# Block-sparse attention and a feed-forward layer on one core: a new issue order from a planner, with four token groups turned through DRAM instead of five and the weights loaded earlier

## The chip, the cores and the metric

The kernel runs on one core of one Trainium2 chip. The metric is the device time of one execution in microseconds (us). Engines are named as in the profile: PE multiplies matrices (PEld loads its stationary operand), DVE and ACT work on vectors, POOL is GpSimd, SP issues most DMAs.

## The reference

Four batches, eight heads, 768 tokens, 64 values per head. Attention is restricted to chunks of 32 keys: for each query the six chunks with the largest upper bound on the score are kept, then causally masked. The attended tokens (3072 of 512 values) go through a feed-forward layer of width 2048.

```python
k_min, k_max = k_chunks.min(axis=3), k_chunks.max(axis=3)
ub = sum(maximum(q * k_min, q * k_max), axis=-1)      # one bound for each query and chunk
ub = where(causal, ub, -1e9)
top_chunks = argsort(ub)[..., -6:]
scores = where(sel & causal_by_token, scale * q @ k.T, -1e9)
x = softmax(scores) @ v                               # tokens x (heads * 64)
h = x @ w_in                                          # 512 -> 2048
out = (h * clip(h + 3, 0, 6) / 6) @ w_out             # 2048 -> 512
```

## The kernel before

**Tiling.** Attention is done in 16 units: unit n has four heads of batch n // 4 (two "pairs" of heads) and one half of its tokens, 384. Units n % 4 of 0 and 1 are the first half, 2 and 3 the second. Two units make one group (batch, half) of 384 tokens, and the dense layers run on the eight groups (0,0), (0,1), (1,0) ... (3,1).

**A unit, in the kernel's names.** K and Q come in as `KS` and `QS`. In batch 0 they are loaded by quads (L237, rows of 256 bytes and more) and turned by PE into `KT`, `QT` (L377), which ACT, DVE and POOL copy out (`KL`, `QF`, L262 to L266). In the other batches four loads each (`load`, L246, rows of 128 bytes) put 32 x 32 blocks where DVE can turn them: `KF`, `QF` (L389). DVE reduces keys to chunk limits `KMA` (L402, L403), PE multiplies them with the queries into bounds `UBT` (L442), DVE turns these (`UB`, L447), finds the six largest (L459), builds the selection `SELA` (L464) and turns it to `MT` (L472), which is put beside the queries in `QLA` by L262 or L264. PE makes the scores `SPS` (L495 in batch 0, L498 after it), ACT the exponentials `PT` (L508), POOL cuts the triangle (L513), PE multiplies with the values `VB` into `PVP` (L529), and DVE divides by the sum (`RINV` L535, `Xb` L541). Values are loaded as `VS` (L252, batch 0) or `VT` (L257) and cast to `VB`.

**Turning the tokens.** The dense layer wants `Xb` with the model dimension on the partitions, as `XT`. There are two ways. By PE: 12 transposes into `XTP` (L550) and two DVE copies (L554). Through DRAM, for the groups in the list `WORDS`: two DVE transposes of pairs of bf16 as fp32 words (`BT`, L560), a store to DRAM (`BD`, L565), four loads (`BF`, L571), all issued by SP, and four POOL copies (L579).

**The dense layers.** `hidden` (L586): 16 steps of 4 matmuls into a bank `HP`; ACT makes `U` (L591), DVE makes `GT` (L594). `result` (L601): for each of three token tiles 16 matmuls into `OP`, then ACT or DVE scale to `OT` (L627, L629) and SP stores (L633). The last tile is done in two halves of columns (L609, L616, L622). `WIN` and `WOUT` (2 MB each in bf16, kept in SBUF) come in two halves each, `WIN0`, `WIN1`, `WOUT0`, `WOUT1`, by DMAs that POOL issues (L325, L328); before each one POOL copies one element of another load's tile (`seen`, L322), so that the load goes out only after that one has landed. The table `GATE` says which.

**What sets the order.** Nothing above is issued where it is written. Each step is given to a planner (`class Plan`) with an engine or a choice of engines, a length, a rank, the steps that it needs and the buffers that it takes and gives. `Plan.order` plays the schedule through, event by event, and each free engine takes the ready step of the lowest rank for which a buffer is free. The instructions are then issued in that order, engine by engine, and no engine changes its order at run time. The rank of a step is a formula in its unit or group plus an entry for that step's number in `SHIFT`. `FETCH` is a time at which the planner adds a delay to a DMA under way. For PE steps before 45 us of the plan in front of which PE stands idle in the plan, a few matmuls on the identity are put in ("fillers", L214).

```python
step = dict(..., rank=(rank + SHIFT.get(len(self.steps), 0), len(self.steps)), ...)
...
for st in sorted(steps, key=lambda x: x["rank"][:1] if e == "DMA" else x["rank"]):
```

Inputs of batch 0 are issued in the order `SEQ` (K0 Q0 K1 Q1 Q3 Q2 K2 V1 V0 V2 K3 V3, by unit). Loads on SP and stores on SP share one queue, whose instructions go out in the planned order too: a store that waits for its result holds the loads behind it.

Of the kernel before, what the change touches and what calls it, by code (L numbers as in the profile page):

```python
# [46 lines left out]
class Plan:  # L47
# [8 lines left out]
    FETCH = 15.3, 1.35  # L56
# [36 lines left out]
    def order(self, **busy):  # L93
# [20 lines left out]
        while events:  # L114
            now, _, done, own = heapq.heappop(events)
            if done:
                behind(done, own)
                if not own:
                    for held in done["give"]:
                        held[1] -= 1  # L120
                        if not held[1]:
                            self.room[held[0]].append(held[2])
                            opened[held[0], held[2]] = now
            for e, steps in ready.items():
                if free[e] > now + 1e-9:
                    continue
                for st in sorted(steps, key=lambda x: x["rank"][:1] if e == "DMA" else x["rank"]):
                    if "engine" in st:
                        steps.remove(st)
                    elif self.sooner(st, e, free, now):  # L130
                        continue
                    elif self.room_for(st):
                        steps.remove(st)
                        for held in st["take"]:
                            held[2] = self.take(held[0])
                        st["idle"] = now - max([free[e], *(opened.get((held[0], held[2]), 0.0) for held in st["take"])])
                        out.append(st)
                        begin = now
                        if e == "POOL" or e == "DVE" and st["port"]:
                            begin = max(now, port["DVE" if e == "POOL" else "POOL"])  # L140
                            port[e] = begin + st["lengths"][e]
                        begin = max(begin, locks.get(st["lock"], 0.0))
                        if e == "PE":
                            begin += 0.1 * (st["tiles"] != tiles)
                            tiles = st["tiles"]
                        length = st["lengths"][e]
                        if e == "PE" and begin < self.COLD:
                            length *= 1.9
                        if e == "DMA":
                            weights = max(free["WT"] - now, 0.0) + sum(x["lengths"]["WT"] for x in ready["WT"])  # L150
                            length = min(length / st["share"], weights + max(length - st["share"] * weights, 0.0))
                            if now <= self.FETCH[0] < now + length:
                                length += self.FETCH[1]
                        st["at"], st["engine"], st["length"] = begin, e, length
                        free[e] = begin + st["length"]
                        if st["lock"]:
                            locks[st["lock"]] = free[e] + 0.12
                        n += 2
                        heapq.heappush(events, (free[e], n, st, True))
                        heapq.heappush(events, (free[e] + self.BEHIND[e], n + 1, st, False))  # L160
                        break
# [10 lines left out]
def kernel(  # L172
# [345 lines left out]
    WORDS = [(1, 1), (2, 0), (2, 1), (3, 0), (3, 1)]  # L518
# [119 lines left out]
    GATE = dict(I0="V3", I1="I0", O0="K4", O1="I1")  # L638
# [15 lines left out]
    def arrive(engine, issue, length, run, after=(), take=(), parts=1):  # L654
# [3 lines left out]
        for part in range(parts):  # L658
# [6 lines left out]
            if engine == "POOL":  # L665
                issued.append(got)
                got = add("GEN", 1.0, 0, after=[got])
# [5 lines left out]
    def load_input(n, name, after=()):  # L673
# [17 lines left out]
        elif half == 0:  # L691
            got = arrive("SP", 0.6, 1.35, (load, two, name, x), after=after, take=take, parts=4)
# [44 lines left out]
    def prepare(n):  # L737
# [11 lines left out]
        for st in two:  # L749
# [3 lines left out]
            for name, f in (("KS", "kf"), ("QS", "qf")):  # L753
# [3 lines left out]
                if first:  # L757
                    m = bank_of[name] = hold("m", 2 if name == "KS" else 1)
                    here = direct[name] = [add("PE", 0.4, r + lead, later(turn, st, name, half), after=here, take=[m], give=used)]
# [9 lines left out]
            else:  # L769
                masks_beside(p, r)  # L770
                made["K", p, half] = [add(dict(POOL=0.54), None, r + lead + 1, later(keys, st, half, j), port=True,
                                          after=[a] + free.get(("KL", p - 6), []), give=[held["kf"]]) for j in range(2)]
            b1 = add("DVE", 0.95 if first else 0.93, r + lead, later(limits, st, half, 0), after=(direct["KS"] if first else [a]) + free.get(("KM", p - 6), []),
# [11 lines left out]
            chain += [c, add(dict(ACT=0.45, DVE=0.33, POOL=0.6) if first else dict(ACT=0.42), None, r + lead, later(queries, st, half, "relu"), after=[c], port=True,  # L785
# [4 lines left out]
            made["Q", p, half] = [add(dict(POOL=0.54), None, r + lead + 1, later(queries, st, half, j), port=True,  # L790
# [17 lines left out]
    def attend(u):  # L808
# [8 lines left out]
        a = add("DVE", 0.36 if half == 0 else 0.53, r + RANK["sel"], later(select, u), after=[a] + selected.get(half, []), give=[ub], port=True)  # L817
# [3 lines left out]
        for j in range(2 if n >= 4 else 0):  # L821
            mask.append(add(dict(DVE=0.46, ACT=0.83, POOL=0.9), None, r + RANK["sel"] + j, later(masks_out, u, j), port=True,
# [3 lines left out]
        for i, st in enumerate(two):  # L826
# [6 lines left out]
            for t in range(tiles):  # L833
# [12 lines left out]
                for jb, q0, w, c0 in PLAN[half][t]:  # L846
                    if q0 == jb * P:
                        parts.append(add("POOL", 0.37, r + RANK["tri"], later(triangle, st, half, t, c0), after=[e]))
# [43 lines left out]
    for what in ("I0", "I1", "O0", "O1"):  # L892
        name, n = dict(I="WIN", O="WOUT")[what[0]], int(what[1])
        got, seen = landing[GATE[what]]
        there[name, n] = arrive("POOL", 0.95, 6.3 if name == "WIN" else 7.3, (load_weights, name, n, seen), after=got[-1:])
# [3 lines left out]
    for n_group, ((b, half), xs) in enumerate(finished.items()):  # L899
# [3 lines left out]
        if (b, half) in WORDS:  # L903
# [12 lines left out]
            for kt in range(KT_HID):  # L916
                xt.append(add("POOL", 0.55, r + RANK["rw"], later(part_words, g, kt), after=landed + xt[:1], take=[held_xt] if kt == 0 else [], give=[held_bf]))
# [6 lines left out]
        for f in range(FT):  # L924
# [3 lines left out]
            a = add("ACT", 0.48, r + RANK["fs"] * f + RANK["rt"], later(hidden_relu, g, f), after=before, take=[u])  # L928
            gts.append(add("DVE", 0.475, r + RANK["fs"] * f + RANK["rt"], later(hidden_out, g, f), after=[a], give=[m, u]))
# [59 lines left out]
```

## Time and profile before

| | |
|---|---|
| time, median of 3 runs | 270.9 us (270.15 to 272.08) |
| profiled execution: time, span | 270.71 us, 269.0 us |
| mean granted clock of PE | 0.998 |
| busy: PE, DVE, ACT, POOL | 258.5, 205.2, 190.0, 125.6 us |
| matmuls of `hidden` and `result` | 512 (L586), 350 + 32 half-width (L601, L609) |
| DMA | 34.91 MB in 115329 packets, of which 100960 under 512 bytes |
| HBM | 29.23 MB read, 8.26 MB written |

Of one execution the span is the time from the first to the last instruction; 1.7 us of the device time lie around it. The matmuls are pipelined, so the busy time of PE counts an instruction from its start to its modelled end. A packet under 512 bytes is a row of one of the input loads for the most part. The chain that ended last goes through PE for 73% of the span.

### The profile page before, as it was taken

What the parts mean: (1) busy time and instruction counts of PE and PEld (TensorE: products, weight loads), DVE (VectorE), ACT (ScalarE), POOL (GpSimd) and SP (SyncE); (2) the same over time, 40 slices, a digit from 0 to 9 for tenths busy, and PEclk for the clock granted to TensorE, in tenths of its full rate; (3) what the DMA queues carried; (4) which work ended last, traced back from release to release, by engine and by line L of the source; (5) the groups of instructions that cost most, each with busy time, mean ns of one, the idle gap of its engine ahead of it and who ended that gap; (6) DMA issues with size and microseconds to landing.
All of it is one profiled execution on the core that took longest, in us unless ns stands there. A gap on an engine that the chain in (4) does not pass through costs nothing.

```text
span 269.0 us, 6720 instructions
## 1 busy us (share of the span) xinstructions
PE 258.5 (96%) x2466; PEld 155.2 (58%) x2484; DVE 205.2 (76%) x582; ACT 190.0 (71%) x305; POOL 125.6 (47%) x284
## 2 busy tenths in 40 slices
PE   7998999999999999899999999999999999999994
PEld 5855666665445666554664566644666556645553
DVE  5789889889988698799889999979997126804800
ACT  3777899686457788764994499944997679716810
POOL 2547577005958559648845584772372221111000
PEclk9999999999999999999999999999999999999999
DMA  7999999999982999994999799223100420042012
GB/s 222 286 208 177 176 180 193 200 131 146 221 208 84 145 177 168 132 175 138 140 143 167 178 130 174 54 80 117 40 0 4 156 80 1 2 157 80 0 39 78
DMA packets 115329, 34.91 MB, mean 130 GB/s; under 512 B 100960, under 2 KB 110688, under 8 KB 115296
## 3 DMA queue, kind: packets, MB, share of 16 engines
q1 hardware_dynamic: 111616, 29.89, 60.3%
q0 software_dynamic: 3136, 4.19, 9.5%
q8 instruction: 19, 0.31, 0.5%
q10 hardware_dynamic: 544, 0.39, 0.5%
q14 instruction: 14, 0.11, 0.1%
HBM read 29.23 MB, written 8.26 MB: 139 GB/s over the span
## 4 chain that ended last, share of the span: by engine, by line
PE 73%; DVE 8%; DMA 7%; ACT 4%; SPq 3%; issue 1%; POOL 1%; ACTq 0%; DVEq 0%; POOLq 0%
PE OP L601 24%; PE HP L586 23%; PE SPS L498 6%; DMA KS<-in_k_dram 5%; PE PVP L529 5%; PE UBT L442 5%; PE SPS L495 3%; DVE GT L594 3%; ACT PT L508 3%; PE QT L377 2%; PE KT L377 2%; SPq L246 2%; PE OP L609 1%; DVE KF L389 1%; DMA BD<-BT 1%
## 5 line engine op out<-in xcount | busy, mean ns | idle before, releaser
L508 ACT ACTIVATE PT<-SPS 128x1024 bf16<-128x1024 f32 (+2 forms) x96 | 84.5, 927 | 11.6 <-PE SPS L498 7.9
L586 PE MATMUL HP<-XT,WIN 128*128 128x384 bf16 x512 | 90.1, 326 | 1.3 <-DVE Xb L541 0.8
L594 DVE SCALAR_TENSOR_TENSOR GT<-U,HP 128x384 bf16<-128x384 bf16 x128 | 67.2, 549 | 29.9 <-ACT U L591 25.6
L601 PE MATMUL OP<-WOUT,GT 128*128 128x512 bf16 x350 | 83.4, 379 | 1.2 <-issue 0.3
L591 ACT ACTIVATE U<-HP,THREE 128x384 bf16<-128x384 f32 x128 | 71.6, 594 | 8.1 <-PE HP L586 4.2
L586 PEld LDWEIGHTS <-WIN 128*128 128x128 bf16 x512 | 48.8, 98 | 32.6 <-issue 1.3
L513 POOL TENSOR_SCALAR_AFFINE_SELECT PT<-PT 128x256 bf16<-128x256 bf16 x96 | 39.6, 423 | 51.5 <-ACT PT L508 50.7
L601 PEld LDWEIGHTS <-GT 128*128 128x128 bf16 x368 | 34.7, 98 | 40.4 <-issue 3.7
L340 POOL TENSOR_SCALAR_AFFINE_SELECT QLA<-QF 64x384 bf16<-64x384 f32 x48 | 24.2, 506 | 24.6 <-DVE QF L389 18.9
L498 PE MATMUL SPS<-QLA,KL 128*128 128x384 bf16 (+2 forms) x240 | 35.5, 278 | 0.1
L627 ACT ACTIVATE OT<-OP 128x512 f32<-128x512 f32 x22 | 13.1, 594 | 30.0 <-PE OP L601 26.7
L498 PEld LDWEIGHTS <-KL 128*128 128x128 bf16 x240 | 21.4, 98 | 12.1 <-issue 0.3
L340 POOL TENSOR_SCALAR_AFFINE_SELECT KL<-KF 64x384 bf16<-64x384 f32 x48 | 24.1, 504 | 8.3 <-DVE KF L389 6.7
L529 PEld LDWEIGHTS <-PT 128*128 128x128 bf16 x672 | 24.3, 97 | 6.0 <-POOL PT L513 2.4
L529 PE MATMUL PVP<-VB,PT 128*128 128x65 bf16 x672 | 26.3, 193 | 1.2 <-POOL PT L513 1.1
L413 ACT ACTIVATE QR<-QF 128x384 f32<-128x384 f32 x29 | 14.5, 525 | 10.4 <-DVE QF L389 8.5
L541 DVE TENSOR_TENSOR Xb<-PVP,RINV 128x384 bf16<-128x384 f32 x32 | 18.5, 579 | 1.1
L579 POOL COPY XT<-BF 128x384 bf16<-128x384 bf16 x20 | 9.7, 523 | 14.9 <-DMA BF<-BD 14.8
L389 DVE STREAM_TRANSPOSE KF<-KS 128x384 f32<-128x384 f32 x24 | 13.2, 560 | 3.3 <-DMA KS<-in_k_dram 3.3
L266 POOL TENSOR_SCALAR_AFFINE_SELECT VB<-VT 128x768 bf16<-128x768 f32 x12 | 10.8, 908 | 6.4 <-DMA VT<-in_v_dram 4.3
L389 DVE STREAM_TRANSPOSE QF<-QS 128x384 f32<-128x384 f32 x24 | 12.3, 550 | 1.7 <-PE UBT L442 1.7
L402 DVE TENSOR_REDUCE KMA<-KF 128x12 f32<-128x384 f32 x24 | 13.1, 547 | 0.5
(75 smaller groups left out, 223.6 us busy)
## 6 DMA issues: line engine op xcount, KB each, us to landing
KS<-in_k_dram SPq DMA_DIRECT2D x31, 192.0 KB, 5.2
QS<-in_q_dram SPq DMA_DIRECT2D x31, 192.0 KB, 5.5
out_dram<-OT SPq DMA_DIRECT2D x23, 256.0 KB, 2.2
VT<-in_v_dram SPq DMA_DIRECT2D x24, 192.0 KB, 4.6
WIN<-in_moe_w_in_dram POOLq DMA_DIRECT2D x2, 1024.0 KB, 9.3
WOUT<-in_moe_w_out_dram POOLq DMA_DIRECT2D x2, 1024.0 KB, 13.0
BD<-BT SPq DMA_DIRECT2D x5, 384.0 KB, 2.3
BF<-BD SPq DMA_DIRECT2D x20, 96.0 KB, 2.3
```

The costliest lines, as they stand in the source:

```text
L340: nc.gpsimd.affine_select(out=to, in_=x, pattern=[[0, n]], compare_op=A.is_ge, fill=0.0, base=0, channel_multiplier=0)
L389: nc.vector.transpose(T[:], st[name][:, st["i"], half * HC:(half + 1) * HC, :].rearrange("p c e -> p (c e)"))
L413: nc.scalar.activation(QR[:], QF[:], ACT.Relu)
L498: nc.tensor.matmul(SP[:, j, c0:c0 + n], lhsT=KLS[st["pair"] % 6][:, j, jb * P:(jb + 1) * P], rhs=st["QL", half][:, j, at:at + n], start=Tr ...
L508: nc.scalar.activation(PT[:, :, 0:cols], SP[:, :, 0:cols], ACT.Exp, scale=scale)
L513: nc.gpsimd.affine_select(out=PT[:, :, c0:c0 + P], in_=PT[:, :, c0:c0 + P], pattern=[[0, 2], [1, P]], compare_op=A.is_ge, fill=0.0, base=0 ...
L529: nc.tensor.matmul(PVP[:, j, n, :], lhsT=PT[:, j, c0:c0 + P], rhs=st["VB"][:, jb, j, :], start=(jb == 0), stop=(jb == qb))
L541: nc.vector.tensor_tensor(out=to, in0=PVP[:, :, :, 0:D], in1=RINV[:].to_broadcast([P, 2, HB, D]), op=A.mult)
L586: nc.tensor.matmul(HP[:], lhsT=WIN[:, kt, f * P:(f + 1) * P], rhs=g["XT"][:, kt, :, :], start=(kt == 0), stop=(kt == KT_HID - 1))
L591: nc.scalar.activation(U[:], g["HP", f][:], ACT.Relu, bias=THREE[:], scale=1.0)
L594: nc.vector.scalar_tensor_tensor(out=g["GT"][:, f, :], in0=g["U", f][:], scalar=6.0, in1=g["HP", f][:], op0=A.min, op1=A.mult)
L601: nc.tensor.matmul(g["OP", t][:], lhsT=g["GT"][:, f, t * P:(t + 1) * P], rhs=WOUT[:, f, :], start=(f == 0), stop=(f == FT - 1))
```

## The change

The kernel computes the same, with the same kinds of instructions, and only three things in its program are set anew:

- `WORDS`: group (1,1) no longer goes through DRAM but by PE (12 transposes, two copies on DVE). The four groups (2,0), (2,1), (3,0) and (3,1) go through DRAM as before.
- `GATE`: the first half of `WIN` waits for unit 1's keys and no longer for unit 3's values; the second half waits for unit 1's values and no longer for the first half; the first half of `WOUT` waits for unit 3's queries and no longer for unit 4's keys; the second half of `WOUT` waits for the first half of `WIN` and no longer for the second.
- The planner's model: lengths of many steps, the times in `FETCH` (four in place of one), and a wholly new table `SHIFT`. These change the order on every engine and queue, the engine that takes a copy where there is a choice, and the fillers: there are 4 in place of 9.

In the diff the table is cut to its ends.

```diff
@@ -25,22 +25,24 @@
 SHIFT = {
-    4: -131.1, 6: -28.5, 8: -992.6, 10: -1029.4, 12: -898.6, 16: -956, 20: -2022.3, 22: -19.7, 24: 1108.1, 34: 1041.4, 36: 1044.5, 40: 1189.7, 42: 1103,
-    46: 1088.3, 48: 1102.1, 75: 80.5, 77: -940.3, 84: -1978.1, 90: 140.1, 98: 100.7, 99: 89.9, 104: -1979.6, 111: -99.4, 133: 34.1, 134: 65.5, 161: 165.8,
...
-    -2035.4, 1422: -1112.9, 1425: -14.9, 1428: -1095.3, 1431: -1036.5, 1433: 1935.8, 1434: 19.9, 1440: 83.6, 1441: 2024.9, 1449: -216.6, 1450: -82.7,
-    1451: -12.7, 1452: -96.7, 1458: -64.7, 1459: -32.2, 1463: -1149.6, 1466: -56.1, 1510: 84.1, 1522: 31.9, 1551: -124.5
+    8: -731.2, 10: -883.5, 12: -875.2, 14: 60.4, 16: 101, 24: 1053.3, 30: 905.2, 32: 974.2, 36: 869.8, 40: 1056.6, 42: 945.6, 46: 977.2, 75: 11.5, 79:
+    -2136.2, 85: -2049.9, 128: -3082.6, 135: -47.7, 159: 221.1, 160: 336.5, 166: 79.4, 170: 134.7, 174: -1917.7, 179: 542.9, 180: -1840, 182: -1863, 183:
...
+    -13.7, 1445: -1996.6, 1451: -288.9, 1454: -193
@@ -53,7 +55,7 @@
-    FETCH = 15.3, 1.35
+    FETCH = 11.5, 59.5, 76.0, 92.0
@@ -149,8 +151,9 @@
-                            if now <= self.FETCH[0] < now + length:
-                                length += self.FETCH[1]
+                            for fetch in self.FETCH:
+                                if now <= fetch < now + length:
+                                    length += 1.2
@@ -515,7 +518,7 @@
-    WORDS = [(1, 1), (2, 0), (2, 1), (3, 0), (3, 1)]
+    WORDS = [(2, 0), (2, 1), (3, 0), (3, 1)]
@@ -635,7 +638,7 @@
-    GATE = dict(I0="V3", I1="I0", O0="K4", O1="I1")
+    GATE = dict(I0="K1", I1="V1", O0="Q3", O1="I0")
@@ -664,7 +667,7 @@
-                got = add("GEN", 1.0, 0, after=[got])
+                got = add("GEN", 1.1, 0, after=[got])
@@ -689,7 +692,7 @@
-            got = arrive("SP", 0.6, 1.35, (load, two, name, x), after=after, take=take, parts=4)
+            got = arrive("SP", 0.6, 1.4, (load, two, name, x), after=after, take=take, parts=4)
@@ -756,7 +759,7 @@
-                    here = direct[name] = [add("PE", 0.4, r + lead, later(turn, st, name, half), after=here, take=[m], give=used)]
+                    here = direct[name] = [add("PE", 0.65, r + lead, later(turn, st, name, half), after=here, take=[m], give=used)]
@@ -768,9 +771,9 @@
-                made["K", p, half] = [add(dict(POOL=0.54), None, r + lead + 1, later(keys, st, half, j), port=True,
+                made["K", p, half] = [add(dict(POOL=0.5), None, r + lead + 1, later(keys, st, half, j), port=True,
-            b1 = add("DVE", 0.95 if first else 0.93, r + lead, later(limits, st, half, 0), after=(direct["KS"] if first else [a]) + free.get(("KM", p - 6), []),
+            b1 = add("DVE", 0.97 if first else 0.93, r + lead, later(limits, st, half, 0), after=(direct["KS"] if first else [a]) + free.get(("KM", p - 6), []),
@@ -782,12 +785,12 @@
-            chain += [c, add(dict(ACT=0.45, DVE=0.33, POOL=0.6) if first else dict(ACT=0.42), None, r + lead, later(queries, st, half, "relu"), after=[c], port=True,
+            chain += [c, add(dict(ACT=0.45, DVE=0.33, POOL=1.05) if first else dict(ACT=0.42), None, r + lead, later(queries, st, half, "relu"), after=[c], port=True,
-            made["Q", p, half] = [add(dict(POOL=0.54), None, r + lead + 1, later(queries, st, half, j), port=True,
+            made["Q", p, half] = [add(dict(POOL=0.5), None, r + lead + 1, later(queries, st, half, j), port=True,
@@ -814,12 +817,12 @@
-        a = add("DVE", 0.36 if half == 0 else 0.53, r + RANK["sel"], later(select, u), after=[a] + selected.get(half, []), give=[ub], port=True)
+        a = add("DVE", 0.4 if half == 0 else 0.6, r + RANK["sel"], later(select, u), after=[a] + selected.get(half, []), give=[ub], port=True)
-            mask.append(add(dict(DVE=0.46, ACT=0.83, POOL=0.9), None, r + RANK["sel"] + j, later(masks_out, u, j), port=True,
+            mask.append(add(dict(DVE=0.36, ACT=0.82, POOL=0.8), None, r + RANK["sel"] + j, later(masks_out, u, j), port=True,
@@ -845,7 +848,7 @@
-                        parts.append(add("POOL", 0.37, r + RANK["tri"], later(triangle, st, half, t, c0), after=[e]))
+                        parts.append(add("POOL", 0.39, r + RANK["tri"], later(triangle, st, half, t, c0), after=[e]))
@@ -892,7 +895,7 @@
-        there[name, n] = arrive("POOL", 0.95, 6.3 if name == "WIN" else 7.3, (load_weights, name, n, seen), after=got[-1:])
+        there[name, n] = arrive("POOL", 1.05, 6.95 if name == "WIN" else 7.4, (load_weights, name, n, seen), after=got[-1:])
@@ -914,7 +917,7 @@
-                xt.append(add("POOL", 0.55, r + RANK["rw"], later(part_words, g, kt), after=landed + xt[:1], take=[held_xt] if kt == 0 else [], give=[held_bf]))
+                xt.append(add("POOL", 0.47, r + RANK["rw"], later(part_words, g, kt), after=landed + xt[:1], take=[held_xt] if kt == 0 else [], give=[held_bf]))
@@ -925,8 +928,8 @@
-            a = add("ACT", 0.48, r + RANK["fs"] * f + RANK["rt"], later(hidden_relu, g, f), after=before, take=[u])
-            gts.append(add("DVE", 0.475, r + RANK["fs"] * f + RANK["rt"], later(hidden_out, g, f), after=[a], give=[m, u]))
+            a = add("ACT", 0.49, r + RANK["fs"] * f + RANK["rt"], later(hidden_relu, g, f), after=before, take=[u])
+            gts.append(add("DVE", 0.48, r + RANK["fs"] * f + RANK["rt"], later(hidden_out, g, f), after=[a], give=[m, u]))
```

27 rows, old and new, of the table SHIFT are left out of this document.

## The prediction

> **What bounds the kernel now.** I read the page's busy times first, then the table by stretches, then what PE waited for, then the timelines at the places found.
>
> ```profile
> PE 258.5 (96%) x2466; PEld 155.2 (58%) x2484; DVE 205.2 (76%) x582; ACT 190.0 (71%) x305; POOL 125.6 (47%) x284
> ```
>
> PE bounds the kernel, and what can be won is only what PE loses. The rows by stretches (columns: window, its length, busy time of PE, PEld, DVE, ACT, POOL, granted clock, DMA share, GB/s) show where:
>
> ```profile
> 0.00:10.00 10.00, 8.43 (x107) 6.76 (x111) 6.50 (x20) 5.26 (x10) 3.65 (x18) 1.00 0.87 256
> 20.00:30.00 10.00, 8.76 (x142) 5.10 (x135) 8.72 (x38) 8.34 (x14) 6.93 (x18) 1.00 1.15 189
> 90.00:100.00 10.00, 9.36 (x106) 6.49 (x104) 8.31 (x19) 8.82 (x11) 4.69 (x12) 1.00 1.20 155
> 100.00:110.00 10.00, 9.16 (x109) 6.28 (x107) 7.30 (x16) 9.00 (x15) 6.99 (x16) 1.00 1.01 162
> 110.00:120.00 10.00, 8.90 (x73) 5.04 (x74) 9.90 (x23) 5.71 (x11) 6.08 (x15) 1.00 1.15 154
> 260.00:270.00 10.00, 5.02 (x40) 3.61 (x37) 0.00 (x0) 1.25 (x3) 0.00 (x0) 0.89 0.17 62
> ```
>
> Busy time counts a stretched pipeline as busy, so I laid the matmuls of the order end to end at the cadence of undisturbed runs, as in these rows of the chain (start, length, what):
>
> ```profile
> 50.54 0.67 PE XTP L550 x12
> 158.11 1.30 PE HP L586 x8
> 151.78 1.73 PE OP L601 x8
> 16.79 0.39 PE UBT L214 x5
> 265.11 0.66 ACT L616 ACTIVATE OT<-OP 128x256 f32<-128x256 f32 x2 [2.94 <-PE OP L609]
> ```
>
> One HP is 0.1625 us, one OP 0.216; with the other kinds the sum from the first matmul ends at 257.2. The last one ended at about 265.1, when ACT took it, so 7.9 us are lost. Comparing the two clocks along the order: 3.3 us are gone by 36, next to nothing until 92, 4.0 between 92 and 113, 0.6 in the rest. Behind the last matmul lie 3.9 us of copy, store and landing, which do not change.
>
> The early loss sits where ACT has no free time:
>
> ```profile
> 24.00:28.00 4.00, 2.76 (x50) 1.82 (x47) 3.93 (x11) 4.00 (x8) 3.61 (x10) 1.00 1.15 177
> 26.01 0.34 PE L495 MATMUL SPS<-MT,EB 64*128 64x384 bf16 x2 [1.04 <-ACT PT L508]
> ```
>
> ACT is busy for 4.00 of 4 us and PE waits for its exponentials to give a bank back. The loss at 92 to 113 has another cause. PE's own waits name POOL and DVE; DVE in turn waits for keys, and these are late since SP was held:
>
> ```profile
> PE SPS L495 <- ACT PT L508: 1.2, 2, 1.0
> PE PVP L529 <- POOL PT L513: 1.1, 2, 0.6
> PE HP L586 <- DVE Xb L541: 0.8, 1, 0.8
> ```
> ```profile
> 93.81 0.58 DVE L389 STREAM_TRANSPOSE KF<-KS 128x384 f32<-128x384 f32 x1 [0.90 <-DMA KS<-in_k_dram]
> 109.14 0.58 DVE L389 STREAM_TRANSPOSE KF<-KS 128x384 f32<-128x384 f32 x1 [2.38 <-DMA KS<-in_k_dram]
> ```
> ```profile
> 76.64 8.95 SPq L633 DMA_DIRECT2D out_dram<-OT  x3
> 85.68 3.75 SPq L246 DMA_DIRECT2D KS<-in_k_dram  x4
> 100.46 4.18 SPq L246 DMA_DIRECT2D KS<-in_k_dram  x3
> ```
>
> Three stores keep SP for 8.95 us; unit 8's keys go out behind them at 85.68 and are waited for until 93.81. The next keys end at 104.6 and are waited for until 109.14. DVE stands for 3.3 us in these two waits, and everything it owes PE (GT, Xb) comes later.
>
> **The change part by part.** The sum is made against the profiled 270.7; the median shown is 270.9, so 0.2 is added at the end.
>
> *PE's own work.* Group (1,1) adds 12 transposes: +0.67. Fillers go from nine to four: five of them took 0.39, so -0.4. That is +0.3, all on PE's path; a longer filler list or a shorter one would give 0 to +0.7. DVE swaps two word transposes for two copies, nearly even, POOL loses four copies and SP a store and four loads:
>
> ```profile
> L554 DVE COPY XT<-XTP 128x768 bf16<-128x768 bf16 x6 | 3.1, 547 | 0.0
> L560 DVE STREAM_TRANSPOSE BT<-Xb 128x384 f32<-128x384 f32 x10 | 5.8, 576 | 0.3
> L579 POOL COPY XT<-BF 128x384 bf16<-128x384 bf16 x20 | 9.7, 523 | 14.9 <-DMA BF<-BD 14.8
> ```
>
> *The first 36 us.* ACT's list in the tight stretch is about 1.0 us longer than before (ten KL, seven QF, seven QR and three VB copies where nine, seven, five and four stood). And WIN's first half, which was issued at 22.1, now goes out behind the second unit's keys, at about 9 to 10, beside nine loads of values and the last keys:
>
> ```profile
> L325 POOL DMA_DIRECT2D WIN<-in_moe_w_in_dram x2: 793/896/1000, 22.1 to 32.9; - x2
> DMA to landing us min/median/max: 8.7/9.3/9.9
> ...
> q0 software_dynamic: 3136, 4.19, 9.5%
> ...
> 7.25 0.51 POOL L266 TENSOR_SCALAR_AFFINE_SELECT KL<-QF 128x384 bf16<-128x384 f32 x1 [5.04 <-ACT QF L262]
> ...
> L252 SPq DMA_DIRECT2D VS<-in_v_dram x12: 368/584/1366, 7.3 to 19.8; - x12
> ...
> DMA to landing us min/median/max: 2.8/4.6/6.2
> ...
> 27.64 0.55 ACT L262 CAST VB<-VS 128x384 bf16<-128x384 f32 x1
> ...
> 15.12 0.54 PE SPS L495 x8
> ...
> 12.00:16.00 4.00, 4.00 (x72) 3.49 (x70) 3.65 (x17) 2.61 (x6) 1.05 (x2) 1.00 1.19 206
> ```
>
> The four halves took 9.5% of 269 us of 16 engines, 25.6 us, so 6.4 each. The engines are already full at 12 to 16 (share 1.19), so 6.4 us of weights push the other loads of that time back. The last values were issued at 19.8, landed 4.6 to 6.2 later and were cast at 27.64: some 2.4 us early. By the count of bytes the first unit's values land at about 21 to 22 (they are wanted at 21), the second's at 26 (wanted at 25). ACT would stand for 0.5 to 2 us where nothing hides it; against that, the first HP of the dense layer, after 31.4 us of undisturbed PE work before, now stands after 30.7. On POOL the copy that waits for the keys and the 0.9 us of the issue stand in front of the first casts of KL, which then begin at about 9.4 and not at 7.25; PE's first scores stood at 15.12, so this costs nothing unless the landing slips by as much. Bounds: -0.5, if the copies just fit and the new order feeds ACT better; +4.0, if the whole 6.4 us reach ACT less the some 2.4 us by which the values were early. I take +0.9.
>
> *36 to 75 us.* The other three halves go out back to back at 27 to 31, 19 us of engine time, in front of the next batch's keys:
>
> ```profile
> L246 SPq DMA_DIRECT2D KS<-in_k_dram x24: 384/1206/9926, 20.5 to 155.8; - x24
> ...
> DMA to landing us min/median/max: 3.1/5.1/21.2
> ...
> DMA to landing us min/median/max: 11.9/13.0/14.1
> ...
> 62.85 1.46 PE L601 MATMUL OP<-WOUT,GT 128*128 128x512 bf16 x5
> ```
>
> With weights under way a load of keys took up to 21.2 us to land (the first landing row; the second is WOUT's) and held SP for 9.9. In the new order the first KF of batch 1 stands behind four copies of the first group at about 39, and the first OP stands at about 51 where it stood at 62.85 before, so WOUT's second half is wanted at about 53; by 27 + 19 plus landing it comes at 50 to 53. Bounds 0 and +3; both look just met, I take +0.4.
>
> The Trainium skill ("DMA: Bandwidth & Descriptors", section "Queues, rings and completion order") says that a DMA engine takes turns between the queues that have work, a packet at a time. The landing of 21.2 us beside the median of 5.1 agrees. By it the values at 10 to 20 us would not stand behind the weights but share with them, each load lasting about twice as long: that is the +4.0 end, which is the second rival.
>
> *80 to 115 us.* Unit 8's keys are issued behind two stores whose results come sooner, three of the four parts after the second of them; at about 155 GB/s and 196 KB a load they land at 92 to 94.5, while the KF that wants them stands at 92 and has the copies of XT ahead of it, so that no HP hangs on it. Unit 9's land at about 104.5, wanted at 104 and harmless until 105.7. So nearly all of the 4.0 should come back: bounds -4.0 and +1 (the stores slip as before and the word chain no longer covers it); I take -3.0.
>
> *115 to 178 us.* The DVE load by PE time stays near one (9.90 of 10 at 110 to 120), now without 4 us of slippage to absorb it: in the new order the first selection of unit 9 reaches QLA about 0.6 before PE wants it, where it had 3.4. Bounds 0 and +2; I take +0.8.
>
> *The end.* The chains through DRAM are hidden by the work in front of them:
>
> ```profile
> 234.27 0.58 DVE L560 STREAM_TRANSPOSE BT<-Xb 128x384 f32<-128x384 f32 x1
> 241.20 1.85 POOL L579 COPY XT<-BF 128x384 bf16<-128x384 bf16 x4 [9.26 <-DMA BF<-BD]
> ```
>
> From BT's start to the last XT are 8.8 us. In the new order the chains of (2,0), (3,0) and (3,1) end 1 to 2 us before the first HP that needs them; what covers them are OP and HP of the group before. If a chain slipped by 2 it would cost about 1. I take +0.1, bounds 0 and +1.
>
> Sum: 0.3 + 0.9 + 0.4 - 3.0 + 0.8 + 0.1 = -0.5; 270.7 - 0.5 = 270.2, and as a median 270.4.
>
> **The rivals.** *Faster.* The loads still arrive in time early (-0.5), the 4.0 come back whole, and nothing new is late: 270.7 + 0.3 - 0.5 - 4.0 = 266.5, 266.7 as a median. For it: all three terms in between are just met, and the 3.3 us of DVE's waits have one cause, which the order removes. Against it: it needs every one of them.
>
> *Slower, by the weights' early start.* WIN's first half starves the values in the first stage (+4.0) and the other halves delay the next batch's keys (+3.0), the rest as forecast: 270.7 + 0.3 + 4.0 + 3.0 - 3.0 + 0.8 + 0.1 = 275.9, 276.1 as a median. It decides from the point where the first values land after 22, and the first KF of batch 1 after 39. For it: the DMA share of 1.19 and the 21.2 us landing. Against it: the values have their 2.4 us of slack, and the keys of the next batch are issued at 23 to 28, most of them ahead of the three halves. In a sentence of its own: the Trainium skill ("TensorE: Matmul & The Clock Gate", Part 1) states that PE's clock halves after some 3.4 us without work; no stall in the rows here lasts so long and the clock is 1.00, but in this rival a stall could, and would add some 2 us to it.
>
> *Slower, by DVE.* Once the keys come in time, DVE has no idle time in 85 to 130 and its order becomes the bound: only 1.0 of the 4.0 comes back and 2.0 are lost behind 115. That is 270.7 + 0.3 + 0.9 + 0.4 - 1.0 + 2.0 + 0.1 = 273.4, 273.6 as a median. For it: 9.90 of 10 us. Against it: DVE idles 2.7 us in 100 to 110, a good part of it in the one wait of 2.38.
>
> **How the numbers follow.** The forecast has 0.36 (its own range 268.2 to 272.5), faster 0.30, the weights 0.18, DVE 0.16. A measurement can tell 1% from no change here, 2.7 us: below 268.2 is faster, above 273.6 slower. Faster: all of its rival and 0.04 of the forecast, 0.34. Slower: 0.16 of the weights' case, 0.08 of DVE's and 0.04 of the forecast, 0.28. The rest, 0.38, is the same. The range runs from 266.4 to 275.8: it leaves out a little below the faster rival's time and the upper half of the weights' case.
>
> **What would show it.** Right: no wait of DVE's KF for KS above 1 us at 85 to 110, PE busy over 9.7 there, PE at 20 to 30 at or below 8.8, XT after its BF without a wait of HP. Wrong: an ACT wait for VS or a PE wait on SPS of more than 2 us before 36, an OP or HP waiting for WOUT or WIN, KF waiting for KS at 36 to 45; or DVE at 10 of 10 with PE waiting for GT in 85 to 130.

## The result: 4.75% slower, and the profile after

The changed kernel takes 284.42 us (median of 4 runs, 283.45 to 284.47) beside 271.49 us for the kernel before in the same comparison; the ratio is 1.0475, with a 95% interval of 1.0425 to 1.0525. The profiled execution took 284.47 us and its span is 282.8 us. Nearly all of the loss is one stall. Rows by stretches of the changed kernel (window, its length, busy time of PE, PEld, DVE, ACT, POOL, granted clock, DMA share, GB/s):

```profile
20.00:30.00 10.00, 8.51 (x148) 6.23 (x144) 9.47 (x34) 9.44 (x15) 7.99 (x20) 1.00 0.66 123
...
40.00:50.00 10.00, 2.26 (x20) 1.22 (x21) 0.00 (x0) 3.05 (x5) 0.00 (x0) 0.84 1.32 198
50.00:60.00 10.00, 4.95 (x26) 2.24 (x26) 7.33 (x16) 2.52 (x3) 4.92 (x13) 0.50 1.04 151
...
100.00:110.00 10.00, 9.41 (x106) 6.18 (x104) 8.76 (x41) 9.84 (x15) 5.91 (x14) 1.00 0.99 164
110.00:120.00 10.00, 10.00 (x120) 7.07 (x118) 9.20 (x21) 9.69 (x16) 6.79 (x15) 1.00 0.95 145
120.00:130.00 10.00, 10.00 (x106) 6.67 (x104) 9.90 (x22) 9.33 (x17) 6.52 (x17) 1.00 1.26 141
```

DVE and POOL do nothing at all in 40 to 50 and PE works for 2.26 us, while the DMA engines are full (share 1.32). Work begins again after 50 with the clock at 0.50. The stretch where the kernel before lost 4.0 us lies at about 105 to 127 in this execution and is nearly whole. The waits of DVE and PE name the stall, and the timelines of DVE and PE place it:

```profile
DVE KF L392 <- DMA KS<-in_k_dram: 14.1, 1, 14.1
PE HP L589 <- DVE GT L597: 12.8, 1, 12.8
```
```profile
52.61 1.04 DVE L392 STREAM_TRANSPOSE KF<-KS 128x384 f32<-128x384 f32 x2 [14.07 <-DMA KS<-in_k_dram]
55.05 1.44 PE L589 MATMUL HP<-XT,WIN 128*128 128x384 bf16 x4 [12.79 <-DVE GT L597]
```

The first KF of batch 1 stands at 38.5 in DVE's order and waits 14.1 us for its keys. The GT copies behind it are late by as much, the banks of HP stay full, and PE stands for 12.8 us. SP's timeline and its own waits say why the keys are late, and POOL's timeline what was issued in the meantime:

```profile
24.07 0.45 SPq L249 DMA_DIRECT2D KS<-in_k_dram  x1
29.38 0.32 SPq L249 DMA_DIRECT2D QS<-in_q_dram  x1
29.75 19.02 SPq L249 DMA_DIRECT2D KS<-in_k_dram  x3
```
```profile
SPq L249 <- POOL seenWOUT L325: 4.8, 1, 4.8
```
```profile
27.74 0.79 POOL L328 DMA_DIRECT2D WIN<-in_moe_w_in_dram  x1
...
29.18 0.17 POOL L325 COPY seenWOUT<-QS 1x1 f32<-1x1 f32 x1
29.30 0.90 POOL L331 DMA_DIRECT2D WOUT<-in_moe_w_out_dram  x1
30.20 0.17 POOL L325 CAST seenWOUT<-WIN 1x1 f32<-1x1 bf16 x1
30.32 0.88 POOL L331 DMA_DIRECT2D WOUT<-in_moe_w_out_dram  x1
```

Two things meet. First a hold: the new gate of WOUT's first half lets POOL copy one element of unit 3's queries, and SP's first load of the next queries goes into that buffer, so SP waits 4.8 us for POOL's copy; three of the four loads of keys stand behind it. The planner knows nothing of this edge. Second the crowding: when these loads go out, from 29.75, three halves of weights have been issued or are about to be, and SP needs 19.02 us to issue three loads. The keys came when the weights were through.

Laid end to end as in the prediction, PE's order needs 0.15 us more than before. PE's loss against it, by stretch (each stretch read off the same instruction in both clocks):

| stretch | before | after | difference |
|---|---|---|---|
| to the first HP, about 36 | 3.3 | 3.9 | +0.6 |
| from there to where unit 8's keys are due | 0 | 15.6 | +15.6 |
| the stretch of unit 8's and 9's keys (92 to 113 before) | 4.0 | 1.1 | -2.9 |
| the rest | 0.6 | 1.0 | +0.4 |

With the 0.15 the differences make 13.8 us, the difference of the two profiled executions (284.47 - 270.71). Of the 15.6, 12.8 are the wait and about 2.7 are the slow clock behind it (rows in the section on the hardware).

### The profile page after: what moved, and what is told of

Its sections match the earlier page's. It is cut to its first block, busy times and chain, and to the rows that moved or that the text cites. A ratio compares the mean times of both kernels' runs of the same rounds, so it can differ in the third digit from the quotient of the medians.

```text
span 282.8 us, 6732 instructions
## 1 busy us (share of the span) xinstructions
PE 262.2 (93%) x2491; PEld 156.8 (55%) x2491; DVE 207.4 (73%) x589; ACT 189.4 (67%) x305; POOL 117.9 (42%) x273
## 3 DMA queue, kind: packets, MB, share of 16 engines
q1 hardware_dynamic: 110896, 29.11, 53.6%
## 4 chain that ended last, share of the span: by engine, by line
PE 79%; SPq 6%; DMA 5%; ACT 5%; DVE 2%; issue 1%; POOL 0%; ACTq 0%; DVEq 0%
PE OP L604 28%; PE HP L589 27%; PE SPS L501 9%; PE PVP L532 6%; SPq L249 5%; PE UBT L445 4%; DMA KS<-in_k_dram 4%; ACT PT L511 2%; PE KT L380 2%; PE QT L380 1%; PE OP L612 1%; DMA VS<-in_v_dram 1%; PE SPS L498 1%; ACT U L594 1%; PE XTP L553 1%
## 5 line engine op out<-in xcount | busy, mean ns | idle before, releaser
L589 PE MATMUL HP<-XT,WIN 128*128 128x384 bf16 x512 | 91.6, 330 | 12.9 <-DVE GT L597 12.8
L604 PE MATMUL OP<-WOUT,GT 128*128 128x512 bf16 x368 | 85.3, 379 | 0.0
L516 POOL TENSOR_SCALAR_AFFINE_SELECT PT<-PT 128x256 bf16<-128x256 bf16 x96 | 38.8, 418 | 55.2 <-ACT PT L511 54.5
L501 PE MATMUL SPS<-QLA,KL 128*128 128x384 bf16 (+2 forms) x240 | 36.2, 278 | 0.6 <-ACT PT L511 0.4
L630 ACT ACTIVATE OT<-OP 128x512 f32<-128x512 f32 x23 | 13.7, 598 | 30.5 <-PE OP L604 26.4
L501 PEld LDWEIGHTS <-KL 128*128 128x128 bf16 x240 | 21.3, 98 | 14.1 <-issue 2.4
L532 PE MATMUL PVP<-VB,PT 128*128 128x65 bf16 x672 | 25.6, 193 | 0.3 <-ACT VB L265 0.3
L416 ACT ACTIVATE QR<-QF 128x384 f32<-128x384 f32 x31 | 15.8, 527 | 13.5 <-DVE QF L392 13.3
L392 DVE STREAM_TRANSPOSE KF<-KS 128x384 f32<-128x384 f32 x24 | 13.2, 560 | 14.1 <-DMA KS<-in_k_dram 14.1
L538 DVE RECIPROCAL RINV<-PVP 128x6 f32<-128x6 f32 x32 | 5.9, 184 | 11.3 <-PE PVP L532 11.2
L405 DVE TENSOR_REDUCE KMA<-KF 128x12 f32<-128x384 f32 x24 | 13.1, 545 | 0.5
L406 DVE TENSOR_REDUCE KMA<-KF 128x12 f32<-128x384 f32 x24 | 13.0, 542 | 0.0
```

What stands on the lines that cost most here:

```text
L392: nc.vector.transpose(T[:], st[name][:, st["i"], half * HC:(half + 1) * HC, :].rearrange("p c e -> p (c e)"))
L416: nc.scalar.activation(QR[:], QF[:], ACT.Relu)
L501: nc.tensor.matmul(SP[:, j, c0:c0 + n], lhsT=KLS[st["pair"] % 6][:, j, jb * P:(jb + 1) * P], rhs=st["QL", half][:, j, at:at + n], start=Tr ...
L516: nc.gpsimd.affine_select(out=PT[:, :, c0:c0 + P], in_=PT[:, :, c0:c0 + P], pattern=[[0, 2], [1, P]], compare_op=A.is_ge, fill=0.0, base=0 ...
L532: nc.tensor.matmul(PVP[:, j, n, :], lhsT=PT[:, j, c0:c0 + P], rhs=st["VB"][:, jb, j, :], start=(jb == 0), stop=(jb == qb))
L589: nc.tensor.matmul(HP[:], lhsT=WIN[:, kt, f * P:(f + 1) * P], rhs=g["XT"][:, kt, :, :], start=(kt == 0), stop=(kt == KT_HID - 1))
```

## The experiments

The two theories after the first look: the **hold** makes the keys late, or the **crowding** by the weights does, whatever SP's queue does.

**Without the hold.** The gate of WOUT's first half reads another tile; the order on every engine stays.

```diff
         got, seen = landing[GATE[what]]
+        if what == "O0":
+            seen = landing["V1"][1]
```

> One read is changed: before WOUT's first half POOL copies an element of unit 1's values (long there) in place of unit 3's queries. The order on every engine stays that of the changed kernel. Theory 'hold': SP's load of the next queries goes into the buffer that POOL's copy still reads, waits 4.8 us for it, and holds three loads of keys behind the weights; without the read these go out at 24.5 to 28 and land at 30 to 34. DVE's KF waits under 1 us for KS (14.1 in the changed kernel), PE's HP under 1 us for GT (12.8), the clock stays at 1.00 and the time is 268 to 271 us. Rival 'crowding': the three halves of weights fill the DMA engines whatever SP does; the keys come about 5 us sooner, KF still waits 7 to 10 us and the time is 277 to 281 us.

Measured: 282.49 us (281.67 to 283.05, 4 runs), ratio to the kernel before 1.0438 (1.0398 to 1.0478). DVE's timeline, PE's, and the times from issue to landing of KS (the least, the median, the most):

```profile
50.25 1.04 DVE L392 STREAM_TRANSPOSE KF<-KS 128x384 f32<-128x384 f32 x2 [11.71 <-DMA KS<-in_k_dram]
...
52.70 1.44 PE L589 MATMUL HP<-XT,WIN 128*128 128x384 bf16 x4 [10.43 <-DVE GT L597]
...
DMA to landing us min/median/max: 3.0/5.2/21.0
```

The keys were all issued by 31.6 and still came at about 50, when WOUT (issued until 31.2, the last landing after 19.3 us) was through. The hold is worth some 2 us: 1.9 by the medians (284.42 - 282.49) and 2.4 by KF's wait (14.07 - 11.71), but the intervals of the two ratios overlap. The theory that made it the cause has fallen, and crowding was worse than its own expectation (a wait of 7 to 10, and 277 to 281 us).

**WOUT later, the hold kept**, and **both**. WOUT's two transfers are issued behind the first two casts of batch 1's keys.

```diff
-            nc.gpsimd.dma_start(WOUT[...], moe_w_out[...])
+            held_back.append(lambda: nc.gpsimd.dma_start(WOUT[...], moe_w_out[...]))
...
         cast(e, KLS[...], st["KS", half, "F"][...], HS)
+        cast_keys[0] += 1
+        while cast_keys[0] == 2 and held_back:
+            held_back.pop(0)()
```

> The copies that gate WOUT stay where they are, so the hold on SP stays too; only the two transfers of WOUT are issued later on POOL, behind the first two casts of batch 1's keys. Theory 'hold' alone: the keys are still issued from 29.7 and KF waits nearly as long as in the changed kernel, over 10 us, and the time stays over 280. Rival 'crowding' alone: with WIN's second half only beside them the keys land by about 40 and KF waits under 3 us. If both are needed for the stall, KF waits 1 to 4 us. In the last two cases WOUT may then come late instead, for the first OP at about 52 to 56: the time would be 270 to 276 us.

> The two edits together: no hold on SP, and WOUT's transfers behind the first casts of batch 1's keys. Both theories: no wait of KF for KS above 1 us before 45. If the transfers of WOUT were what crowds, this beats the kernel without the hold alone; if they were not, it is the same or slower by what OP waits for WOUT: 268 to 272 us.

Measured: 276.45 us with the hold, 272.72 us without it (one run each). DVE's and PE's timelines, with the hold first:

```profile
42.18 1.04 DVE L394 STREAM_TRANSPOSE KF<-KS 128x384 f32<-128x384 f32 x2 [4.01 <-DMA KS<-in_k_dram]
...
61.71 1.02 PE L609 MATMUL OP<-WOUT,GT 128*128 128x512 bf16 x4 [3.80 <-DMA WOUT<-in_moe_w_out_dram]
```
```profile
39.35 1.04 DVE L394 STREAM_TRANSPOSE KF<-KS 128x384 f32<-128x384 f32 x2 [0.57 <-DMA KS<-in_k_dram]
...
57.46 1.02 PE L609 MATMUL OP<-WOUT,GT 128*128 128x512 bf16 x4 [2.38 <-DMA WOUT<-in_moe_w_out_dram]
```

WOUT's early transfers are the larger part: without them the wait for keys falls from 14.07 to 4.01, and without the hold too to 0.57. What is left of the loss without the hold is the wait for WOUT, which is now too late; with the hold PE also waits 2.9 us in all for GT. The wait of 4.01 is at the edge of what was expected for the case that both are needed, and both times lie just above their ranges (276 and 272).

**What the crowding is.** The same kernel without the hold, with the three late halves in shorter rows, and a control with as many transfers but rows as long as before.

```diff
-            nc.gpsimd.dma_start(WIN[:, :, c0:c1], ...)
+            step = 256 if part else 1024                  # short rows: by columns
+            for c in range(c0, c1, step):
+                nc.gpsimd.dma_start(WIN[:, :, c:c + step], ...)
...
-            nc.gpsimd.dma_start(WOUT[:, ft:ft + FT // 2, :], ...)
+            for c in (slice(0, DMODEL // 2), slice(DMODEL // 2, DMODEL)):
+                nc.gpsimd.dma_start(WOUT[:, ft:ft + FT // 2, c], ...)
```
```diff
+            step = 1 if part else 4                       # the control: by rows
+            for x in range(0, 4, step):
+                nc.gpsimd.dma_start(WIN[:, x:x + step, c0:c1], ...)
...
+            for x in (ft, ft + FT // 4):
+                nc.gpsimd.dma_start(WOUT[:, x:x + FT // 4, :], ...)
```

> The kernel without the hold, with the three late halves of weights in rows of 1 KB of the input (WIN in four pieces by columns where one transfer had rows of 4 KB; WOUT in two where one had 2 KB); bytes are the same. Theory 'turns by packet': a row of keys waits for one row of weights at a time, so shorter rows let the keys through sooner: 160 turns become 384 while the weights run. KF waits for KS 3 to 6 us (11.7 without the hold and with long rows) and the time is 273 to 278 us. Rival 'the keys come when the weights are through, whatever the rows': KF waits over 10 us, the time stays at 281 to 285 us.

> The control for the kernel with short rows: the three late halves in the same number of transfers, cut by rows, so that each row stays as long as it was. Both theories: KF waits as without the hold, 9 to 13 us, and the time is 280 to 285 us. If it falls as with the short rows, the number or the issue times of the transfers were the cause and not the length of the rows.

Measured: 274.20 us with short rows, 282.10 us in the control (one run each). DVE's timeline and the landings of KS, short rows first:

```profile
43.09 1.03 DVE L395 STREAM_TRANSPOSE KF<-KS 128x384 f32<-128x384 f32 x2
...
DMA to landing us min/median/max: 3.0/5.3/13.6
```
```profile
49.02 1.04 DVE L395 STREAM_TRANSPOSE KF<-KS 128x384 f32<-128x384 f32 x2 [8.84 <-DMA KS<-in_k_dram]
...
DMA to landing us min/median/max: 3.0/5.1/19.9
```

The bytes are the same and the number and times of the issues nearly so, yet the keys are there at 43.09 at the latest, not at 49.02. KF does not wait at all with short rows, where 3 to 6 us were expected, but in part because DVE itself comes to it 2.9 us later than in the control (49.02 - 8.84 = 40.18): POOL needs 6.58 us to issue the three halves in short rows and 5.20 in the control, and its triangles wait meanwhile. In the control KF waits a little less than expected (9 to 13). The packets that each queue moved from 40 to 44 (packets, MB, share of 16 engines) show what happens; first the run without the hold, then the control, then the short rows:

```profile
q0 software_dynamic: 655, 0.65, 107.6%
q1 hardware_dynamic: 656, 0.08, 26.2%
...
q0 software_dynamic: 762, 0.76, 111.6%
q1 hardware_dynamic: 763, 0.10, 31.1%
...
q0 software_dynamic: 1342, 0.67, 122.2%
q1 hardware_dynamic: 1344, 0.17, 54.7%
```

q0 carries the weights and q1 what SP issues. In these rows they move packet for packet, whatever the length of the weights' rows, and with rows of 1 KB SP's queue gets twice as many turns as with the rows of the run without the hold. The length of the weights' rows decides how long the keys take. The Trainium skill ("DMA: Bandwidth & Descriptors", section "Queues, rings and completion order") says that the DMA engines take turns between queues at packet granularity; these two runs agree.

**The gates of before in the changed kernel.** The planner orders anew.

```diff
-    GATE = dict(I0="K1", I1="V1", O0="Q3", O1="I0")
+    GATE = dict(I0="V3", I1="I0", O0="K4", O1="I1")
```

> The changed kernel with the four gates of the kernel before (WIN behind unit 3's values and behind its own first half, WOUT behind unit 4's keys and WIN's second half); lengths, ranks and the list of groups stay those of the change, and the planner orders anew. Both theories: no hold and no crowding before 36, so no wait of KF above 2 us before 60. Theory that the gates alone cost the time: 267 to 271 us. Rival, that the new ranks cost by themselves: over 273.

Measured: 287.59 us (286.05 to 288.19, 4 runs), ratio 1.0622 (1.058 to 1.0664). ACT's and POOL's timelines:

```profile
28.06 0.51 ACT L265 CAST VB<-VS 128x384 bf16<-128x384 f32 x1 [7.44 <-DMA VS<-in_v_dram]
...
18.52 0.92 POOL L328 DMA_DIRECT2D WIN<-in_moe_w_in_dram  x1
```

The expectation for the keys held: KF does not wait for KS. The time is not at 267 to 271 but over 273, as the rival had it, though it is not shown to be so for the rival's reason. The run doesn't price the gates alone: with these ranks WIN's first half goes out at 18.52, just ahead of the last values, and ACT waits for these until 28.06, about when WIN lands. That looks like the same crowding at another place, in the first stage, and PE stands there for 6.9 us; the run loses PE time in later stretches too, and what each gate is worth stays open.

**The list of groups alone.** In the kernel before, group (1,1) is turned by PE, and the later ranks are kept on their steps.

```diff
-    WORDS = [(1, 1), (2, 0), (2, 1), (3, 0), (3, 1)]
+    WORDS = [(2, 0), (2, 1), (3, 0), (3, 1)]
```

> The kernel before with one edit: group (1,1) is turned by PE and not through DRAM; the ranks of all later steps are kept. By the prediction's terms this adds 0.67 us of transposes to PE and takes four copies from POOL, one store and four loads from SP: 270 to 272.5 us, within 1% of the kernel before. Rival, that DRAM for this group was what delays the keys at 92 to 113: 267 to 269 us.

Measured: 282.43 us (282.03 to 283.89, 4 runs), ratio 1.0436 (1.0398 to 1.0474). DVE's and PE's timelines:

```profile
108.76 0.58 DVE L390 STREAM_TRANSPOSE KF<-KS 128x384 f32<-128x384 f32 x1 [3.15 <-DMA KS<-in_k_dram]
...
254.18 12.55 PE L587 MATMUL HP<-XT,WIN 128*128 128x384 bf16 x64 [3.13 <-POOL XT L580]
```

The rival has fallen: the keys are waited for just as before, so it was not the group's way through DRAM that delayed them. The forecast of no change has fallen too. PE loses in several places: in 160 to 180 it is busy 18.01 of 20 us (19.89 in the kernel before), in 240 to 260 16.75 (19.95), where the last chain through DRAM is no longer covered. That the planner's order behind the group, another one with the old ranks, is the reason was not tested. What the list costs with ranks that suit it stays open.

**WOUT at 36.** No hold, and WOUT's transfers behind POOL's triangle at 36: the edit of "both", but counted by triangles.

```diff
-        while cast_keys[0] == 2 and held_back:
+        while cast_keys[0] == 18 and held_back:      # counted in triangle()
```

> No hold, and WOUT's two transfers behind POOL's triangle at about 36 (they went out at 41 to 43 with the next casts of keys, and OP waited 2.4 us for them). Turns by packet: the keys have landed but for a few rows when WOUT's begin, so KF waits under 2 us, and WOUT comes 4 to 5 us sooner, so OP waits under 0.5: 269 to 271.5 us. Rival: the first rows of WOUT catch the last keys again and KF waits over 4 us: 273 to 277.

Measured: 269.85 us (269.45 to 270.61, 10 runs), ratio to the kernel before 0.9964 (0.9947 to 0.998). One of its waits and rows of its stretches:

```profile
DVE KF L394 <- DMA KS<-in_k_dram: 0.6, 1, 0.6
```
```profile
90.00:100.00 10.00, 9.42 (x118) 6.86 (x117) 8.24 (x19) 9.56 (x14) 5.88 (x13) 1.00 1.27 161
100.00:110.00 10.00, 10.00 (x116) 6.92 (x115) 9.90 (x23) 9.50 (x16) 6.09 (x15) 1.00 1.30 131
110.00:120.00 10.00, 10.00 (x88) 5.94 (x87) 9.86 (x24) 6.21 (x11) 8.15 (x20) 1.00 1.09 162
```

KF waits 0.6 us in the whole execution, OP does not wait for WOUT, and with the rest of the change kept the loss of the changed kernel is gone (14.6 us less). Against the kernel before it is 0.36% faster at the median; the interval leaves out 1, but the ranges of the two overlap (269.45 to 270.61 and 270.33 to 271.83), so this is hardly a gain.

**Unit 8's keys late again**, in this last kernel: three of their four loads are moved behind six other loads on SP.

```diff
+        if name == "KS" and two is units[8][0] and part:
+            late_keys.append(go)
+            return
         go()
+        if name == "QS" and two is units[8][0] and part == 1:
+            while late_keys:
+                late_keys.pop(0)()
```

> The kernel with WOUT's transfers at about 36, and one more move on SP: three of the four loads of unit 8's keys go out behind four loads of values and two of queries, about 5 to 7 us later, so that they come as late as in the kernel before. Theory that these keys cost the kernel before its 4.0 us at 92 to 113: KF waits 4 to 7 us for KS there, PE stands for GT, Xb or PVP behind it, and the time is 272 to 275 us. Rival, that DVE's own work sets that stretch and the keys' wait is absorbed: 269.5 to 271 us.

Measured: 276.87 us (one run), 7.0 more than the median without the move. DVE's timeline, PE's and a row of the stretches:

```profile
102.34 0.58 DVE L403 STREAM_TRANSPOSE KF<-KS 128x384 f32<-128x384 f32 x1 [5.35 <-DMA KS<-in_k_dram]
...
104.48 2.72 PE L603 MATMUL HP<-XT,WIN 128*128 128x384 bf16 x8 [4.52 <-DVE GT L611]
...
100.00:110.00 10.00, 5.52 (x45) 3.56 (x45) 6.68 (x15) 4.38 (x6) 5.71 (x12) 0.66 1.02 139
```

So DVE's own work did not absorb the keys' delay: a wait of 5.35 became 4.52 on PE, and with the clock at 0.66 more than that, so that the time lies 2 us above what was expected. The order of SP around unit 8's keys can cost several us. But the move made these keys later than they were in the kernel before, where KF got them at 93.81 and not at 102.34, so it does not price the 2.9 us that the change gains there.

## Why the prediction was wrong, by its own steps

- *PE's own work*, +0.3: 0.15 by the orders laid end to end. Right.
- *The first 36 us*, +0.9 in bounds of -0.5 to +4.0: +0.6. PE at 20 to 30 is busy 8.51 us, as foretold under 8.8; ACT is busy 9.44 (8.34 before), and its one wait for values there is 0.36 us.
- *36 to 75 us*, +0.4 in bounds of 0 to +3: +15.6. **This is the step that failed**, and it alone put the time outside the range. The mechanism was named (the halves of weights delay the next batch's keys), with its place, the first KF at 39, and a wait of KF for KS at 36 to 45 was among the signs of being wrong; its size was wrong by a factor of five even at the upper bound, and so was the chance of 0.18 for that rival, whose time of 276.1 the result passes by 8 us.
- *80 to 115 us*, -3.0: -2.9. Right, and not by the luck of the stall: the last kernel has no stall, no wait of KF for KS there, and PE is busy 9.42, 10.00 and 10.00 us in the three rows from 90 to 120 (9.36, 9.16 and 8.90 before). That the keys' earlier issue is the whole reason fits this and the move of the keys, but was not tested alone.
- *115 us to the end*, +0.9 together: +0.4. DVE's tighter stretch cost little; that rival did not come.

With the hold and WOUT's early start taken out, the same order takes 269.85 us where the forecast was 270.4, so the other terms hold in sum.

Three things made the size wrong. The prediction priced the weights in engine time, 6.4 us for each half, and gave the keys no price beside them; of the values it said that sharing makes a load last about twice as long. What is shared is turns. The queues' rows of the changed kernel (packets, MB, share of 16 engines) show what a turn is:

```profile
q1 hardware_dynamic: 110896, 29.11, 53.6%
q0 software_dynamic: 3136, 4.19, 8.8%
```

A packet on SP's queue takes 0.022 us of an engine (0.536 x 282.8 x 16 / 110896), one of the weights 0.127. A load of keys is 192 KB in rows of 128 bytes, 96 packets on each of 16 engines: 2.1 us of an engine's time by itself. Beside the weights it gets one packet for each of theirs: 656 in 4 us on 16 engines in the run without the hold are 0.098 us for a pair, so 9.4 us for a load, over four times as long; with short rows 1344 give 0.048 us and 4.6 us. These are estimates from the rows of 40 to 44. In the run without the hold SP's queue passed 320, 706, 656 and 1472 packets in the four stretches of 4 us from 32 to 48, two loads' worth in all, which fits the longest landing of 21.0 us there. The kernel before had shown a landing of 21.2 us, which the prediction quoted, and a load of keys that takes 21 us cannot be there at 39, neither from 29.75 nor from 23 to 28, where the prediction had its issue; the row was read as a worst case when it was the price.

Second, the keys' issue was put at 23 to 28, ahead of the three halves. The hold was overlooked: POOL's gating copy reads the very buffer that the next load writes, which no line of the planner tells. It was worth some 2 us by itself, and 3.7 (276.45 - 272.72) once WOUT was out of the way.

Third, the clock: the prediction kept the Trainium skill's rule on it to a sentence beside the rival, at some 2 us, and the rows below make it 2.7.

## What to carry to other kernels

Price a load beside another queue's transfers by packets, not by bytes: with rows of 128 bytes here and of 2 to 4 KB there, the keys came when the weights were through. When a gate is made by reading a tile, look who writes that tile next: the reader holds the writer's whole queue. And a change whose parts gain a few us in several stretches is decided by the one stretch where a wait has no cover, so the bound of that term needs the longest landing in the trace, not the median.

## What the runs showed of the hardware

The clock after a long stall, in rows of 2 us of the changed kernel:

```profile
42.00:44.00 2.00, 0.26 (x2) 0.03 (x1) 0.00 (x0) 1.18 (x3) 0.00 (x0) 1.00 1.42 210
...
46.00:48.00 2.00, 0.00 (x0) 0.00 (x0) 0.00 (x0) 0.00 (x0) 0.00 (x0) 0.70 1.40 212
48.00:50.00 2.00, 0.00 (x0) 0.00 (x0) 0.00 (x0) 0.00 (x0) 0.00 (x0) 0.50 0.88 131
...
58.00:60.00 2.00, 2.00 (x12) 0.93 (x9) 1.97 (x5) 1.50 (x2) 0.60 (x3) 0.50 0.84 118
60.00:62.00 2.00, 2.00 (x32) 1.37 (x30) 0.59 (x3) 1.18 (x3) 1.11 (x3) 0.89 0.91 137
```

PE stopped at 42.26, and a mean of 0.70 in 46 to 48 puts the fall to half at about 46.8, 4.5 us later. It worked again from 55.05, and 0.89 in 60 to 62 puts the return at about 60.4, 5.4 us later. Those 5.4 us of work at half speed are the 2.7 us that the stall cost beyond its length.

The length of a stall alone does not decide. A stall of 3.80 us (WOUT later, the hold kept) left the clock at 1.00, but one of 3.13 us in the run with the list of groups alone and one of 2.42 us in the run with short rows (PE waits for POOL's triangle there) were followed by a short fall. A row of each, soon after the stall:

```profile
256.00:258.00 2.00, 2.00 (x9) 0.96 (x7) 0.62 (x2) 1.16 (x2) 0.00 (x0) 0.54 0.03 8
...
38.00:40.00 2.00, 2.00 (x8) 0.97 (x7) 0.56 (x2) 1.51 (x2) 0.41 (x1) 0.50 1.79 216
```

The Trainium skill ("TensorE: Matmul & The Clock Gate", Part 1) gives a window of some 3.4 us of idleness or of work for either turn, and says that the window runs freely, so that it does not begin when PE stops. By that a turn comes one to two windows after PE stops or starts, 3.4 to 6.8 us as an estimate from its figure, and the measured 4.5 and 5.4 agree. The stalls of 3.13 and 2.42 us are shorter than one window and do not agree; what decides there no run shows.

The DMA engines took turns between SP's queue and POOL's packet for packet (656 and 655 in 4 us in the run without the hold).
